# Side work of an attention and FFN kernel placed anew among the main matmuls

## The chip, the cores and the metric

The kernel runs on one core of one Trainium2 chip. The metric is the device time of one execution in microseconds (us), given as the median of several runs. The profile is that of one execution; its times are counted from the start of its span.

## What is computed

Eight batches of an attention over 32 learned slots are followed by a bilinear feed-forward layer. The inputs are q, k, v (8 batches, 8 heads, 576 tokens, 64 wide) and phi (8, 8, 576, 32).

```python
a = np.exp(phi - np.max(phi, axis=2, keepdims=True))
a = a / (np.sum(a, axis=2, keepdims=True) + 1e-09)
k_m = np.einsum('bhsm,bhsd->bhmd', a, k)
v_m = np.einsum('bhsm,bhsd->bhmd', a, v)
scores = (1.0 / np.sqrt(64)) * np.matmul(q, k_m.transpose(0, 1, 3, 2))
attn = softmax(scores)                      # over the 32 slots
x = np.matmul(attn, v_m)                    # to (4608, 512): all heads of a token side by side
out = ((x @ w_a) * (x @ w_b)) @ w_out       # 512 -> 1536 -> 512
```

## The kernel before

The kernel never forms x. It multiplies the 32-slot `v_m` of each head into `w_a` and `w_b` first (the "fold"), so that x @ w_a becomes attn times a folded matrix with 256 rows. For one batch the work on TensorE is this:

- **KV sums** (`kv_sums`, L222): 72 small matmuls in tiles of 64 rows and 32 columns add up `k_m`, `v_m` and the denominators, into two PSUM banks. `take_kv` (L242, units km0 and km1) normalises them on VectorE into `rep` and frees the banks; `rep` is transposed by a DMA on the SP queue (`kv_turn`, unit kvd; batches 4 to 7) or by TensorE (unit kvt; batches 2 and 3).
- **Scores** (`scores`, unit sc, L318): 32 matmuls in tiles of 32*32 into four banks, which ScalarE empties with an exponential (`exp_scores`, units e0 and e1, L331).
- **Normalising** the softmax: for batches up to 3 with TensorE sums, a logarithm and an exponential (units den and nr, L341 to L352); for batches 4 to 7 by turning E with a DMA (unit ed), sums and reciprocals on VectorE (sm0, sm1), products on GpSimd and VectorE (tn0, tn1) and turning it back (ad).
- **Fold** (`fold`, L389): for each third of the 1536 columns (v0, v1, v2) and each of the two weight matrices (a, b), 8 matmuls in 64*32 tiles into two banks. `take_fold` (units x0a to x2b, L402) copies one bank on ScalarE and one on VectorE, or both on ScalarE for the middle third of batches 4 to 7, and frees the two banks. Where one unit folds for both matrices, batches 3 to 7 call `work.settle()` first (L383), which pulls products of the down projection for as long as the flag `brim` says that two of its banks are held at once.
- **Up steps** (`up_half`, L652): twelve steps for each half of a batch's tokens. A step has two matmuls for `pa`, copied on ScalarE to `a_sb` (L663), and two for `pb`, multiplied with it on VectorE into `ht` (L666). These are 128*128 tiles.
- **Down products** (`two_downs`, L518): pairs of 128-token chunks are multiplied with `w_out` in seven products of six matmuls each. Their sums `h_sums` are made ahead by GpSimd (L509), for the last two pairs by VectorE. ScalarE and VectorE put the parts together and SP stores them.

The loop over the batches runs the up steps in order. Behind each half-step `ups` (L677) calls `work.advance()`, which pulls down products at the rate that `work.plan` set for the half, and then the next entry of a list of side units written out by hand: `period[b]`, L755 to L760, with 24 entries for the 24 half-steps of batch b. A unit without a mark belongs to batch b + 1, one with `'` to batch b + 2, one with `_` to batch b. An entry "d5" pulls five more down products, "L6" issues the four input loads of batch 6 (phi, k, v, q; L78, L82, L85, L90) on GpSimd's queue, and "-" does nothing. Units joined by "+" run one after the other within an entry. L753 has such a list for the second half of batch 1.

PSUM banks are dealt out in turn by the class `Banks`: `take` gives the bank that was freed or taken longest ago and isn't held. An entry's place thus sets the order of instructions on every engine, and which bank each later tile gets.

Of the kernel before, what the change touches and what calls it, by code (L numbers as in the profile page):

```python
# [18 lines left out]
def kernel(  # L19
# [72 lines left out]
    def load(b):  # L92
        load_phi(b)
        load_k(b)
        load_v(b)
        load_q(b)
# [571 lines left out]
    def up(b, i, hfs):  # L668
        for hf in hfs:
            up_half(b, i, hf, 0)  # L670
        if len(hfs) > 1:
            yield
        for hf in hfs:
            up_half(b, i, hf, 1)
        yield

    def ups(steps, side=()):  # L677

        side = iter(side)
        for step in steps:  # L680
            for _ in up(*step):
                work.advance()
                next(side, us[step[0]]["-"])()
        for f in side:
            work.advance()
            f()
# [5 lines left out]
    def half_steps(b, hf, lo=0):  # L692

        return [(b, i, (hf,)) for i in range(lo, NFF)]
# [10 lines left out]
    def slots(b, names):  # L705

        def both(fs):
            return lambda: [f() for f in fs]
        def unit(n):
            if n == "fin":  # L710
                return lambda: work.pull(-work.done % NFF)
            if n[0] == "L":
                return lambda: load(int(n[1:]))
            if n[0] == "y":
                return lambda: some(int(n[1:]))
            if n[0] == "d" and n[1:].isdigit():
                return lambda: work.pull(int(n[1:]))
            return us[b + n.endswith("'") - n.endswith("_")][n.rstrip("'_")]

        return [both([unit(n) for n in x.split("+")]) for x in names.split()]  # L720
# [3 lines left out]
    def some(n):  # L724
        for _ in range(n):
            next(early, None)
# [23 lines left out]
    ups(steps(1, 0, 4), slots(1, "d3+y1+hv1a+hx1a hv1b+y3+hx1b - - - y3+v1+x1a+x1b - -"))  # L750
    ups(half_steps(1, 0, 4), slots(1, "- v2+x2a+x2b+qt0' - - qt1'+exp0' exp1'+qt2' - kv'+km'+y9"))
    work.plan(S + HALF, 10)
    ups(half_steps(1, 1, 4), slots(2, "- kvt+qt3 - sc+e0+e1 d1 den0+den1+d1+nr0 - v0a+v0b+nr1+x0a x0b - v1+x1b+x1a -"))  # L753
    period = {}
    period[2] = "v2a_+v2b_+d1+x2a_+L4+x2b_+exp0 - - exp1 kv+km+d1+qt0 - qt1+qt2+d7+kvt - L5+qt3+sc+e0 - d2+v0a+v0b+e1+x0a+x0b - den0+exp0'+d2+d4 v1+nr0+x1a x1b+d10+exp1' - - v2+x2a+x2b+kv' den1+km0' - km1'+kvd'+qt0' - nr1+d4 d5+qt1'+qt2'+qt3' - d6"  # L755
    period[3] = "exp0' sc+exp1'+e0+e1+d3+ed v0b+x0b - v0a+x0a+kv'+km0' km1' d2+sm0+sm1 - kvd' d6+d5+tn1 - tn0+ad v1+x1a+d3 - - x1b L6 qt0' v2+d2+x2a+x2b d1+qt1'+qt2' - - - - qt3'"
    period[4] = "exp0' sc+exp1'+e0+e1+d3+ed - v0a+v0b+x0b+x0a+kv'+km0' km1' - kvd'+d4+d5+sm0+sm1 d2 - d3+tn1 - qt0'+tn0+ad d1+v1+x1a+d3 qt1'+L7 - - - x1b v2a+v2b+x2a+x2b - - d2 - - qt2'+qt3'"
    period[5] = "exp0' sc+exp1'+e0+e1+d3+ed - v0+x0b+x0a+kv'+km0' km1' - d7+sm0+sm1 tn0 d3 d1+kvd'+d5+tn1+d3 - - ad+v1+x1a qt0'+x1b - - - v2+x2b - x2a+qt1' - d2 qt2' qt3' -"
    period[6] = "sc e0+e1+ed - v0+x0b - - sm0 x0a+sm1 d2+v1+d6+x1b+tn1 tn0 ad+d6+x1a - d3 - - - d1 v2+x2a - d3 - x2b+d6 -"
    period[7] = ""  # L760
    for b in range(2, B):
        side = slots(b + 1, period[b])
# [33 lines left out]
```

## Time and profile before

| what | value |
|---|---|
| median of 4 runs | 239.69 us (239.4 to 240.01) |
| the profiled execution | 239.49 us |
| its span | 237.7 us |
| granted TensorE clock, mean | 0.998 |
| up matmuls (L655) | 768, 286 ns each by the trace, next start 122 ns later |
| copies of `pa` (L663, ScalarE) | 192, 409 to 415 ns |
| products into `ht` (L666, VectorE) | 192, 447 to 450 ns |
| fold copies (L402, 512 wide) | ScalarE 52 of 604 ns, VectorE 36 of 685 ns |
| `h_sums` (L509, GpSimd) | 56, 1643 ns |
| out stores (SP) | 68 of 128 KB, 2.7 us to landing |

In lines of the timeline, the first number is the start in us, the second the time from the first start to the last end, then engine, line, operation, what is written from what, tile size, shape and how many. Matmuls are pipelined and overlap, so starts are compared and not durations. In the chain of waits a line has start, duration and what the chain passed through.

### The profile page before, as it was taken

Reading aid. Unit: us, or ns where it says so; the run is one execution under the profiler, and the core shown is the slowest. Engines: PE = TensorE matmul, PEld = TensorE weight load, DVE = VectorE, ACT = ScalarE, POOL = GpSimd, SP = SyncE. Lnnn points to the kernel's source line nnn. Section 1 sums busy time; section 2 is a strip of 40 time slices with the busy share of each in tenths; the row PEclk is TensorE's granted clock in tenths of the full one; section 3 lists DMA queues with packets and bytes.
Section 4 is the critical chain, followed back from the end, with each engine's and each line's share of the span. In section 5 each row is a group of like instructions: output and inputs, shape, how many; then the busy total and the mean of one; then the engine's idle time right before and its main releaser. Section 6 shows DMA issues by size and latency. Waiting matters only on the chain.

```text
span 237.7 us, 7716 instructions
## 1 busy us (share of the span) xinstructions
PE 227.8 (96%) x3064; PEld 167.6 (71%) x3064; DVE 168.5 (71%) x415; ACT 154.2 (65%) x394; POOL 154.7 (65%) x132
## 2 busy tenths in 40 slices
PE   7888998999999999999999999999999999999993
PEld 7645563455756867868777877878687778888882
DVE  3646874368949968979785886779676877756642
ACT  2276761569699489796877458877776777565430
POOL 7954244599979949592889959582929265946001
PEclk9999999999999999999999999999999999999999
DMA  6999999999972999953389959997233260122155
GB/s 233 234 197 206 214 249 207 246 217 276 227 176 64 221 268 237 214 114 74 72 215 208 210 115 201 220 178 100 51 92 70 70 132 8 43 49 68 39 116 134
DMA packets 38437, 37.27 MB, mean 157 GB/s; under 512 B 14689, under 2 KB 32481, under 8 KB 38401
## 3 DMA queue, kind: packets, MB, share of 16 engines
q0 software_dynamic: 19264, 23.14, 52.5%
q1 hardware_dynamic: 18624, 12.85, 24.8%
q10 hardware_dynamic: 512, 0.79, 1.0%
q8 instruction: 24, 0.39, 0.7%
q14 instruction: 13, 0.10, 0.1%
HBM read 42.47 MB, written 9.44 MB: 218 GB/s over the span
## 4 chain that ended last, share of the span: by engine, by line
PE 70%; DMA 16%; POOL 7%; ACT 2%; issue 1%; DVE 1%; DVEq 0%; POOLq 0%
PE py L527 16%; PE pa L655 16%; PE pb L655 15%; PE pv L527 8%; DMA wa_sb<-in_moe_w_a_dram 6%; DMA wo_sb<-in_moe_w_out_dram 6%; PE pva L389 4%; DMA kv_sb<-in_v_dram 4%; PE px L527 4%; PE po L451 3%; PE pkv L222 2%; POOL h_sums L509 2%; POOL wb_sb L100 1%; PE pscore L318 1%; POOL wa_sb L99 1%
## 5 line engine op out<-in xcount | busy, mean ns | idle before, releaser
L666 DVE TENSOR_TENSOR ht<-a_sb,pb 128x288 f16<-128x288 f16 x168 | 72.0, 447 | 34.5 <-ACT a_sb L663 27.7
L655 PEld LDWEIGHTS <-vab 128*128 128x128 f16 x768 | 73.0, 98 | 22.3 <-issue 5.2
L663 ACT CAST a_sb<-pa 128x288 f16<-128x288 f32 x168 | 66.2, 409 | 29.2 <-PE pa L655 25.7
L655 PE MATMUL pa<-A,vab 128*128 128x288 f16 x384 | 75.8, 286 | 0.0
L655 PE MATMUL pb<-A,vab 128*128 128x288 f16 x384 | 75.3, 286 | 0.1
L509 POOL TENSOR_TENSOR h_sums<-ht 128x768 f16<-128x768 f16 x28 | 45.9, 1643 | 28.1 <-DVE ht L666 28.1
L527 PEld LDWEIGHTS <-h_sums 128*128 128x128 f16 x384 | 36.9, 98 | 8.7 <-issue 2.5
L402 ACT CAST vab<-pva 128x512 f16<-128x512 f32 (+1 forms) x60 | 32.0, 574 | 9.5 <-PE pva L389 9.3
L527 PEld LDWEIGHTS <-ht 128*128 128x128 f16 x288 | 27.9, 98 | 6.2 <-issue 1.3
L527 PE MATMUL py<-w_sums,h_sums 128*128 128x256 f16 x192 | 30.0, 273 | 0.0
L402 DVE CAST vab<-pva 128x512 f16<-128x512 f32 (+1 forms) x44 | 27.0, 637 | 4.2 <-PE pva L389 4.0
L509 POOL TENSOR_TENSOR h_sums<-h_sums,ht 128x768 f16<-128x768 f16 x14 | 23.0, 1645 | 1.0
L509 POOL TENSOR_TENSOR h_sums<-ht,h_sums 128x768 f16<-128x768 f16 x14 | 23.0, 1642 | 1.0
L331 ACT ACTIVATE E<-pscore 128x288 f16<-128x288 f32 x32 | 10.8, 418 | 11.1 <-PE pscore L318 10.9
L527 PE MATMUL pv<-w_sums,h_sums 128*128 128x256 f16 x96 | 16.5, 273 | 0.0
L527 PE MATMUL py<-w_sums,ht 128*128 128x256 f16 x96 | 16.2, 273 | 0.1
L534 ACT ACTIVATE u<-py 128x256 f32<-128x256 f32 x32 | 12.5, 391 | 5.8 <-PE py L527 5.3
L527 PE MATMUL py<-wo_sb,ht 128*128 128x256 f16 x96 | 15.9, 273 | 0.0
L527 PE MATMUL pv<-wo_sb,h_sums 128*128 128x256 f16 x96 | 14.9, 272 | 0.0
L527 PE MATMUL px<-wo_sb,ht 128*128 128x256 f16 x96 | 14.9, 273 | 0.0
L205 DVE STREAM_TRANSPOSE qT<-q_sb 128x288 f32<-128x288 f32 x32 | 14.2, 460 | 0.1
L196 ACT ACTIVATE exp_sb<-phi_sb 128x576 f16<-128x576 f32 x16 | 10.9, 696 | 5.2 <-DMA phi_sb<-in_phi_dram 5.2
(71 smaller groups left out, 264.7 us busy)
## 6 DMA issues: line engine op xcount, KB each, us to landing
out_dram<-o_sb SPq DMA_DIRECT2D x68, 128.0 KB, 2.7
phi_sb<-in_phi_dram POOLq DMA_DIRECT2D x8, 576.0 KB, 7.9
kv_sb<-in_v_dram POOLq DMA_DIRECT2D x7, 576.0 KB, 11.7
kv_sb<-in_k_dram POOLq DMA_DIRECT2D x7, 576.0 KB, 11.1
q_sb<-in_q_dram POOLq DMA_DIRECT2D x6, 576.0 KB, 14.3
wo_sb<-in_moe_w_out_dram POOLq DMA_DIRECT2D x6, 256.0 KB, 12.8
q_sb<-in_q_dram POOLq DMA_DIRECT2D x4, 288.0 KB, 11.0
wa_sb<-in_moe_w_a_dram POOLq DMA_DIRECT2D x2, 512.0 KB, 13.9
```

Of the source, the lines that this page charges most:

```text
L196: nc.scalar.activation(out=t["exp"][:, 2 * z:2 * z + 2, :, :], in_=phis[b][:, 2 * z:2 * z + 2, :].rearrange("p c (i m) -> p c i m", m=M), ...
L205: nc.vector.transpose(out=t["qT"][:, hp, :].bitcast(F32), in_=qs[b][:, hp, :].bitcast(F32))
L331: nc.scalar.activation(out=Ev[:, g, :, z, :], in_=pss, func=AF.Exp, scale=1.0 / (8.0 * CS))
L389: nc.tensor.matmul(t["pva", lo, z][g][0][32 * j:32 * j + 32, 0:hi - lo], t["kvT"][64 * r:64 * r + 64, 4 + g, M * j:M * j + M], w_sbs[z][64 ...
L402: engine_copy(out=vabs[b][z][:, g, lo:hi], in_=pva[:, 0:hi - lo])
L451: nc.tensor.matmul(po, ht[:, i, P * c:P * (c + 1)], wo_sb[:, i, :], start=(i == 0), stop=(i == NFF - 1))
L509: engine.tensor_tensor(out=out, in0=in0, in1=in1, op=op)
L527: nc.tensor.matmul(po, lhs[:, i], rhs[:, i], start=first and i == 0, stop=i == KH - 1, skip_group_check=not first)
L534: nc.scalar.mul(out=x, in_=po, mul=scale)
L655: nc.tensor.matmul(ps, vabs[b][x][:, g, P * i:P * (i + 1)], attn[b][:, g, HALF * hf:HALF * (hf + 1)], start=(g == 0), stop=(g == 1))
L663: nc.scalar.copy(out=a_sbs[b, i, hf], in_=ps)
L666: nc.vector.tensor_tensor(out=ht[:, i, t0:t0 + HALF], in0=a_sbs.pop((b, i, hf)), in1=ps, op=ALU.mult)
```

## The change

The entries of `period[2]` to `period[6]` and the list at L753 are placed anew. No unit is added and none is dropped; some pairs of half units are written as one (v0a+v0b as v0, v2a+v2b as v2) or the other way, which decides whether `settle` runs before them, and the numbers of down products pulled at single entries differ. Functions are unchanged.

```diff
-    ups(half_steps(1, 1, 4), slots(2, "- kvt+qt3 - sc+e0+e1 d1 den0+den1+d1+nr0 - v0a+v0b+nr1+x0a x0b - v1+x1b+x1a -"))
+    ups(half_steps(1, 1, 4), slots(2, "- kvt+qt3 - sc+e1+e0 - den0+den1+d1+nr0 - v0+nr1+x0a x0b - v1+x1a+x1b -"))
     period = {}
-    period[2] = "v2a_+v2b_+d1+x2a_+L4+x2b_+exp0 - - exp1 kv+km+d1+qt0 - qt1+qt2+d7+kvt - L5+qt3+sc+e0 - d2+v0a+v0b+e1+x0a+x0b - den0+exp0'+d2+d4 v1+nr0+x1a x1b+d10+exp1' - - v2+x2a+x2b+kv' den1+km0' - km1'+kvd'+qt0' - nr1+d4 d5+qt1'+qt2'+qt3' - d6"
-    period[3] = "exp0' sc+exp1'+e0+e1+d3+ed v0b+x0b - v0a+x0a+kv'+km0' km1' d2+sm0+sm1 - kvd' d6+d5+tn1 - tn0+ad v1+x1a+d3 - - x1b L6 qt0' v2+d2+x2a+x2b d1+qt1'+qt2' - - - - qt3'"
-    period[4] = "exp0' sc+exp1'+e0+e1+d3+ed - v0a+v0b+x0b+x0a+kv'+km0' km1' - kvd'+d4+d5+sm0+sm1 d2 - d3+tn1 - qt0'+tn0+ad d1+v1+x1a+d3 qt1'+L7 - - - x1b v2a+v2b+x2a+x2b - - d2 - - qt2'+qt3'"
-    period[5] = "exp0' sc+exp1'+e0+e1+d3+ed - v0+x0b+x0a+kv'+km0' km1' - d7+sm0+sm1 tn0 d3 d1+kvd'+d5+tn1+d3 - - ad+v1+x1a qt0'+x1b - - - v2+x2b - x2a+qt1' - d2 qt2' qt3' -"
-    period[6] = "sc e0+e1+ed - v0+x0b - - sm0 x0a+sm1 d2+v1+d6+x1b+tn1 tn0 ad+d6+x1a - d3 - - - d1 v2+x2a - d3 - x2b+d6 -"
+    period[2] = "v2_+d1+d1+x2a_+x2b_+L4+exp0 - exp1+qt0 - kv+km+qt1+qt2 d4 d7+kvt - L5+qt3+sc+e1+e0 - d2 exp0' den0+d4+v0b+x0b+d2 d1+v1+nr0+x1a x1b+d10+exp1' - - v2+x2a+kv'+x2b+v0a+x0a - den1+km0' km1'+kvd'+qt0'+qt1' nr1 - d5+qt2'+qt3' - d6+d4"
+    period[3] = "exp0' sc+exp1'+e0+e1+d3+ed - v0a+x0a+kv'+v0b+km0' x0b km1' d5+sm0+kvd'+tn0 - - sm1+d6+d5 tn1+ad - v1+x1a+d3 L6 - x1b - qt0' v2+x2a+d2+x2b - - d4 - qt1'+qt2'+qt3' d1"
+    period[4] = "exp0'+d3 sc+exp1'+e0+e1+ed - v0+x0b+x0a+kv'+d4+km0' km1' - kvd'+d5+sm0+tn0 d2 sm1 - d2+tn1+qt0' qt1'+ad v1+x1a+d3 L7 - - x1b - v2+x2a - - - x2b - qt2'+qt3'"
+    period[5] = "exp0' sc+exp1'+e0+e1+ed+d5 - d3 v0a+v0b+x0b+x0a+kv'+km0' - km1' d8+sm0+tn0 - sm1+d3+d5+kvd' - tn1+v1 x1a+d3 qt0'+x1b - qt1'+d2 ad+d6+d3 - v2+x2a+x2b d4 - - qt2' qt3' -"
+    period[6] = "sc e0+e1+ed - - - - - sm0 - sm1+tn0+d2+v0a+v0b+x0a+x0b+v1+d6+x1b d6 d1+d9 x1a+tn1+ad - - - - - - - - v2+x2a+x2b -"
     period[7] = ""
```

## The prediction, made before the changed kernel ran

> **What bounds the kernel now.** First I read the page's table of busy time, the granted clock and the shares of the chain of waits:
>
> ```profile
> span 237.7 us, 7716 instructions
> PE 227.8 (96%) x3064; PEld 167.6 (71%) x3064; DVE 168.5 (71%) x415; ACT 154.2 (65%) x394; POOL 154.7 (65%) x132
> PEclk9999999999999999999999999999999999999999
> PE 70%; DMA 16%; POOL 7%; ACT 2%; issue 1%; DVE 1%; DVEq 0%; POOLq 0%
> ```
>
> The reader sees TensorE busy in 96% of the span, its clock granted throughout, and no other engine above 71%. From 57 us on the kernel is one stream of matmuls. So a change in the order of work can move the time in two ways only: by what TensorE pays at the seams of its own stream, and by the places where the stream stands still. I read both from TensorE's timeline, first where it changes its tile size (batch 4's two half folds of v0, batch 5's sums):
>
> ```profile
> 103.14 0.41 PE L655 MATMUL pb<-A,vab 128*128 128x288 f16 x2
> 103.48 0.41 PE L389 MATMUL pva<-wb_sb,kvT 64*32 64x512 f16 x8
> 103.82 0.42 PE L655 MATMUL pa<-A,vab 128*128 128x288 f16 x2
> 104.08 0.41 PE L655 MATMUL pb<-A,vab 128*128 128x288 f16 x2
> ...
> 105.23 0.41 PE L389 MATMUL pva<-wa_sb,kvT 64*32 64x512 f16 x8
> 105.46 0.95 PE L222 MATMUL pkv<-kv_sb,exp_sb 64*32 64x192 f16 x72
> 106.34 0.42 PE L655 MATMUL pa<-A,vab 128*128 128x288 f16 x2
> ```
>
> Starts are the thing to read, since durations overlap. A pair of up matmuls with its like behind it takes 0.24 us (103.82 to 104.08 less the 0.02 that follows a switch); the pair at 103.14 takes 0.34 to the fold: 0.10 more. A fold of one weight matrix (8 matmuls) followed by work of the same 64*32 size takes 0.23 (105.23 to 105.46); followed by 128*128 work it takes 0.34: 0.11 more. One visit to the small tile size therefore costs 0.20 us beyond its own work, and work joined to a visit costs nothing extra.
>
> Then the stalls in the region that the change touches:
>
> ```profile
> 85.65 0.41 PE L389 MATMUL pva<-wa_sb,kvT 64*32 64x512 f16 x8
> 85.98 0.41 PE L389 MATMUL pva<-wb_sb,kvT 64*32 64x512 f16 x8
> 86.34 0.41 PE L655 MATMUL pa<-A,vab 128*128 128x288 f16 x2
> ...
> 129.60 0.40 PE L389 MATMUL pva<-wb_sb,kvT 64*32 64x512 f16 x8
> 130.17 0.94 PE L222 MATMUL pkv<-kv_sb,exp_sb 64*32 64x192 f16 x72 [0.17 <-DMA kv_sb<-in_v_dram]
> ```
>
> The folds at 85.65 need 0.33 and 0.36 where 0.23 and 0.34 are enough: 0.12 lost. The fold at 129.60 needs 0.57 for 0.23: 0.34 lost, because the sums of batch 6 wait for v. The chain of waits over that stretch says why v is late:
>
> ```profile
> 115.47 1.65 POOL h_sums L509
> 117.19 1.64 POOL h_sums L509
> 118.82 0.76 POOL phi_sb L78
> 119.58 0.74 POOL kv_sb L82
> 120.31 9.72 DMA kv_sb<-in_v_dram
> ```
>
> GpSimd issues batch 6's loads only after two more h_sums operations. Three further stalls, of about 0.5 (four `pD` matmuls at 67.4), 0.54 (a fold pair that takes 69.88 to 70.97, 1.09 us, against 142.11 to 142.66, 0.55, for one that waits for nothing) and 0.1 us (72.4), lie before the point from which the orders differ in substance.
>
> **The change, part by part.** No instruction is added or dropped: 3064 matmuls stand in both orders, and evictions, loads and stores are only permuted. In the built order of TensorE, tile-size changes number 106 before and 104 after.
>
> *Visits.* Batch 4's two half folds of v0, which the fence shows as two visits, now stand before and behind batch 5's sums: one visit fewer. All other visits are merely moved; the half fold v0a of batch 3 too goes to the far side of a KV visit that exists already. Gain 1 x 0.20 = 0.20 us. This is a plain sum, for nothing hides TensorE's seams.
>
> *Load 6.* In GpSimd's order the four DMA issues of batch 6 (L78, L82, L85, L90) now stand behind the first of the three h_sums operations instead of the third. They go out 2 x 1.72 = 3.4 us earlier (115.47 to 118.82). The transfer of v took 9.72 us, so it lands near 126.6 and not 130.04, with the sums still at 130: the 0.34 us go. The two h_sums operations and the fourth go behind the loads, the former by 4 x 0.75 = 3.0 us. Their users have 4.7 us and more of slack (released 117.11 and 118.82, used 122.39 and 123.53), and the fourth, released at 123.47 and used at 124.68, moves little since loads and sums only swap. Cost 0; if that cover were gone, at most 3.0 - 1.2 = 1.8 us. On SP two or four output stores move ahead of the A transposes of batches 6 and 7; these landed 7.96 and 6.84 us before TensorE took them. Batch 5's E transpose landed at 135.78, 0.03 before VectorE took it, while batch 6's loads ran until 134.71; with these earlier it is not later.
>
> *Batch 3's folds at 85.65.* After the change three more half-steps (some 1.5 us of up and down products) follow the scores before a fold, and all four exponentials run in one piece on ScalarE. Four such took 1.32 us at 102.64, a pitch of 0.30; the products after them hide that. The fold finds its banks empty: gain 0.12. The same swap of e0 and e1 in batch 2 makes the first `pD` wait for the last exponential, and only moves part of a wait that the copy of `a_sb` behind them sets anyway: 0.03 lost.
>
> *New waits.* Three places come out short when evictions are laid end to end. Behind each stands all of TensorE's stream. (a) Batch 3's v2 and its v0a, three half folds, are now evicted in a row; VectorE took 1.28 us for two of 0.68 each at 93.62, a pitch of 0.60. Three take 1.88, and the `ht` next in its queue ends some 0.1 us after TensorE wants its bank. I take 0.12 with the ACT copy in the same place; bounds 0 and one `ht`, 0.45. (b) Batch 4's kvT, already binding by 0.11 at 102.15: its last `rep` now has that extra 0.60 eviction ahead, less the 0.26 in which VectorE was idle before and a 0.36 `ht` that moved behind; nearly even. I take 0.04 lost; bounds -0.11 (wait gone) and 0.3. (c) Batch 4's v0b goes behind batch 5's sums, and the next pairs reuse the banks of `pkv`. These come free 2.06 us after the sums start (105.46 to 107.52, the end of the first two `rep` operations) and are handed over 0.05 later; the `pb` of the second half-step wants one after 0.78 (the sums without their switch) + 0.34 + 0.49 + 0.22 + 0.24 = 2.07. I take 0.05; bounds 0 and 0.45.
>
> *The last batch.* v0 and v1 now stand in one slot, yet not in one run. Before a double fold, `settle` pulls products until PSUM is off its brim, and in the built order 11 products stand between the two runs. There are three visits before and after. Gain 0. The folds come 43 matmuls later for v0 and 34 for v2, and the A transpose 34 later, some 4 us. Its landing had 6.84 us to spare, so about 3 remain: cost 0, and if the cover were gone, no more than the 3 us transfer itself.
>
> Sum: -0.20 - 0.34 - 0.12 + 0.03 + 0.12 + 0.04 + 0.05 = -0.42 us. The profiled execution took 239.49 us (span 237.7 and 1.8 around it), so it would come to 239.07; the median of the four runs is 0.20 above it, and the same sum from 239.69 gives 239.27, rounded 239.3 us.
>
> *The skill against the row.* The row says 0.10 us for each change of tile size. The Trainium skill, "TensorEngine Tiling (Array Packing)", Tiling Modes, says that changing the mode drains the TensorE, and "TensorE: Matmul & The Clock Gate", Single matmul latency, puts a warm matmul's constant part near 166 ns. By that, as an estimate, two changes would bring 0.33 us and the sum would be -0.55. The trace's starts decide. Against the change speaks the first page's section Performance Considerations (PSUM Bottleneck): tiling speeds TensorE up but not the emptying of PSUM. Longer runs in small tiles are what it warns of; by it the three new waits would lie at their upper bounds.
>
> **Rivals.** *All stalls go, none comes.* Without the four new losses (0.24) and with the kvT wait of 0.11 gone: -0.20 - 0.34 - 0.12 - 0.11 = -0.77, 238.9 us. For it: the three new waits are each around 0.1, less than a transfer or a queue may shift. Against: VectorE is without idle time around 94 to 98 us.
>
> *The runs wait for PSUM (slower).* A longer run takes up to six banks of eight while two ACT and two DVE copies per pair empty them. Its price is the row at 69.88: 0.54 us a run. Four runs are longer or lie closer (batch 3's v2 with v0a, batch 4's v0 with the sums, batch 7's v0 and v1). Against the 0.66 of gains it decides from the second wait on; with three, 3 x 0.54 - 0.66 = +0.96, 240.65 us. Against it: runs of 16 at 142, 147 and 171 us pass without a wait.
>
> *It does not do what it says.* Only one visit is saved, as counted. If besides v lands no earlier, because the transfer, not the issue, is limited, what is left is -0.42 + 0.34 = -0.08: 239.6 us. For it: the v of batch 5 took 14.7 us from issue to landing, which from 116.9 would be too late. Against it: that one ran behind batch 4's loads; the v of batch 4 took 10.7, and even 12 would be in time.
>
> **How the numbers follow.** About 0.2%, 0.48 us, is what a measurement of this kernel can tell from no change. My forecast, -0.42, has 0.52 and lies just inside that; its own range is 238.9 to 239.6, and a quarter of it (0.13) is beyond -0.48. The first rival has 0.26, the second 0.10, the third 0.12. Faster: 0.13 + 0.26 = 0.39; same: 0.39 + 0.12 = 0.51; slower: 0.10. The range runs from the first rival less the spread of the runs (0.3) to the new waits near their upper bounds (0.45 + 0.3 + 0.45 in place of 0.21 gives +0.57): 238.6 to 240.2.
>
> **What would show it.** The sums of batch 6 0.23 us behind the fold before them, with no wait on in_v; batch 3's folds at 0.23 and 0.34; batch 4's half folds around batch 5's sums with no switch between. A new wait shows as an up pair longer than 0.25 just behind the sums of batches 4 and 5. Wrong I would be if a fold takes 0.5 again past 75 us, if TensorE waits for h_sums near 122, or if batch 7's first up waits for A.

## The result, and the profile after

| kernel | median | runs | lowest to highest |
|---|---|---|---|
| before | 239.73 us | 53 | 239.12 to 240.92 |
| after | 239.11 us | 32 | 238.76 to 240.53 |

The ratio of after to before is 0.9978, with a 95% interval of 0.997 to 0.9986: 0.53 us less, between 0.34 and 0.72. The same kernel run a second time, on another occasion, gave 238.97 us and a ratio of 0.9972 (0.996 to 0.9983). The profiled execution of after took 239.16 us with a span of 237.5; that of before had 239.49 and 237.7. So the two profiles differ by 0.33 where the medians differ by 0.62, and to find out why is the main part of what follows.

The head of the page of after, with the shares of the chain of waits:

```profile
span 237.5 us, 7718 instructions
PE 227.3 (96%) x3064; PEld 167.7 (71%) x3064; DVE 169.5 (71%) x415; ACT 153.5 (65%) x394; POOL 155.6 (66%) x132
PEclk9999999999999999999999999999999999999999
PE 76%; DMA 14%; POOL 5%; ACT 2%; issue 1%; DVE 1%; DVEq 0%; POOLq 0%
```

The same matmuls, the same clock, and busy shares within one point. GpSimd (POOL) has gone from 7% to 5% of the chain, since its loads of batch 6 no longer stand there. The rest is read from TensorE's timeline, first around batch 4's scores and batch 5's sums:

```profile
101.91 0.27 PE L527 MATMUL py<-w_sums,ht 128*128 128x256 f16 x1
102.58 0.48 PE L318 MATMUL pscore<-qT,kvT 32*32 32x288 f16 x32 [0.40 <-DMA kvT<-rep]
...
104.62 0.41 PE L389 MATMUL pva<-wa_sb,kvT 64*32 64x512 f16 x8
104.85 0.97 PE L222 MATMUL pkv<-kv_sb,exp_sb 64*32 64x192 f16 x72
105.59 0.44 PE L389 MATMUL pva<-wb_sb,kvT 64*32 64x512 f16 x8
105.96 0.42 PE L655 MATMUL pa<-A,vab 128*128 128x288 f16 x2
...
106.68 0.41 PE L655 MATMUL pa<-A,vab 128*128 128x288 f16 x2
107.04 0.42 PE L655 MATMUL pb<-A,vab 128*128 128x288 f16 x2
```

Fold, sums and fold are one visit now: 104.62 to 105.96, 1.34 us. Before, the same work took 0.10 (switch) + 0.34 + 0.23 + 0.88 = 1.55 in two visits. That is 0.21 less, as foreseen (0.20). The pair at 106.68 needs 0.36 to its partner where 0.24 is enough: the bank wait (c), 0.11. TensorE's weight loads (PEld) at that place name what ended it, one of VectorE's `rep` operations:

```profile
107.04 0.11 PEld L655 LDWEIGHTS <-vab 128*128 128x128 f16 x2 [0.26 <-DVE rep L254]
```

The wait (a) stands behind batch 3's `pD` matmuls:

```profile
95.36 0.41 PE L341 MATMUL pD<-E,ones 128*128 128x288 f16 x2
95.69 0.41 PE L655 MATMUL pa<-A,vab 128*128 128x288 f16 x2
```

The 0.33 between them is 0.09 more than the 0.24 that is enough; the `ht` operation behind VectorE's three fold copies ended at 95.64, just before. And the scores of batch 4 start 0.67 after the product before them, where a product and a change of size take 0.20: they wait 0.47 for kvT, where before they waited 0.11.

Batch 3's first fold, and the sums of batch 6, in the same view:

```profile
87.52 0.41 PE L389 MATMUL pva<-wb_sb,kvT 64*32 64x512 f16 x8
87.87 0.39 PE L527 MATMUL px<-wo_sb,ht 128*128 128x256 f16 x2
...
129.84 0.40 PE L389 MATMUL pva<-wb_sb,kvT 64*32 64x512 f16 x8
130.05 0.95 PE L222 MATMUL pkv<-kv_sb,exp_sb 64*32 64x192 f16 x72
```

Both stalls are gone: 0.35 to the next work of another size, and 0.21 from fold to sums. For the sums, GpSimd's timeline shows why:

```profile
114.24 1.64 POOL L509 TENSOR_TENSOR h_sums<-ht 128x768 f16<-128x768 f16 x1 [2.28 <-DVE ht L666]
115.82 0.81 POOL L78 DMA_DIRECT2D phi_sb<-in_phi_dram  x1
116.62 0.75 POOL L82 DMA_DIRECT2D kv_sb<-in_k_dram  x1
117.36 0.75 POOL L85 DMA_DIRECT2D kv_sb<-in_v_dram  x1
```

v is issued at 117.36 instead of 120.31. Its transfer took 11.09 us instead of 9.72 and landed at 128.44, 1.61 us before the sums began.

### The profile page after: what moved, and what is told of

Read it like the earlier page. It is cut to its first block, busy times and chain, and to the rows that moved or that the text cites. A ratio compares the mean times of both kernels' runs of the same rounds, so it can differ in the third digit from the quotient of the medians.

```text
span 237.5 us, 7718 instructions
## 1 busy us (share of the span) xinstructions
PE 227.3 (96%) x3064; PEld 167.7 (71%) x3064; DVE 169.5 (71%) x415; ACT 153.5 (65%) x394; POOL 155.6 (66%) x132
## 4 chain that ended last, share of the span: by engine, by line
PE 76%; DMA 14%; POOL 5%; ACT 2%; issue 1%; DVE 1%; DVEq 0%; POOLq 0%
PE py L527 17%; PE pa L655 17%; PE pb L655 17%; PE pv L527 8%; DMA wa_sb<-in_moe_w_a_dram 6%; DMA wo_sb<-in_moe_w_out_dram 6%; PE pva L389 5%; PE px L527 4%; PE po L451 3%; PE pkv L222 2%; DMA kvT<-rep 2%; PE pscore L318 1%; POOL wb_sb L100 1%; POOL wa_sb L99 1%; POOL kv_sb L168 1%
## 5 line engine op out<-in xcount | busy, mean ns | idle before, releaser
L509 POOL TENSOR_TENSOR h_sums<-ht 128x768 f16<-128x768 f16 x28 | 46.7, 1669 | 23.4 <-DVE ht L666 23.4
L527 PE MATMUL px<-wo_sb,ht 128*128 128x256 f16 x96 | 15.9, 273 | 0.0
L527 PE MATMUL py<-w_sums,ht 128*128 128x256 f16 x96 | 15.2, 272 | 0.1
L527 PE MATMUL pv<-wo_sb,h_sums 128*128 128x256 f16 x96 | 14.4, 272 | 0.0
L196 ACT ACTIVATE exp_sb<-phi_sb 128x576 f16<-128x576 f32 x16 | 10.9, 700 | 5.2 <-DMA phi_sb<-in_phi_dram 5.2
```

What stands on the lines that cost most here:

```text
L196: nc.scalar.activation(out=t["exp"][:, 2 * z:2 * z + 2, :, :], in_=phis[b][:, 2 * z:2 * z + 2, :].rearrange("p c (i m) -> p c i m", m=M), ...
L509: engine.tensor_tensor(out=out, in0=in0, in1=in1, op=op)
L527: nc.tensor.matmul(po, lhs[:, i], rhs[:, i], start=first and i == 0, stop=i == KH - 1, skip_group_check=not first)
```

## The experiments

Each row gives the ratio to the kernel before with its 95% interval, from 11 or 12 runs of the kernel. Runs e0, e1, e2 and e4 were measured together on one chip, e3, e5, e6 and e7 on a second, e8 to e10 on a third, e11 on a fourth, each time beside the kernel before; so medians are compared within these groups, and ratios across them.

| run | what | median | ratio |
|---|---|---|---|
| e0_after_again | after, once more | 238.97 | 0.9972 (0.996 to 0.9983) |
| e1_load6_late | after, loads of batch 6 late | 239.71 | 1.0006 (0.9995 to 1.0016) |
| e2_load6_early | before, loads of batch 6 early | 239.22 | 0.9986 (0.9976 to 0.9997) |
| e3_one_visit | before, one visit fewer | 239.77 | 1.0016 (1.0002 to 1.0031) |
| e4_km_early | after, batch 4's rep early | 239.56 | 1.0006 (0.999 to 1.0022) |
| e5_visit_load6 | before, both of e2 and e3 | 239.34 | 0.9993 (0.9984 to 1.0001) |
| e6_last_run | after, last folds really in one run | 240.12 | 1.0024 (1.0015 to 1.0033) |
| e7_scores_later | after, batch 4's scores later | 239.65 | 1.0005 (0.9991 to 1.0019) |
| e8_visit_undone | after, the saved visit undone | 239.23 | 0.9978 (0.996 to 0.9995) |
| e9_q5_late | after, q of batch 5 loaded late | 238.95 | 0.9961 (0.9941 to 0.9981) |
| e10_q_late | as e9, q of batches 6 and 7 too | 239.68 | 0.9995 (0.997 to 1.0021) |
| e11_q5_fill | as e9, products behind the sums | 239.23 | 0.9985 (0.9971 to 0.9998) |

The lists hold 23 to 26 entries; what stands beyond the 24th runs behind the last half-step. To compare profiles, each is cut into stretches by TensorE's starts: from the pair at 58.9 us (up to there all orders are alike) to where batch 4's scores could start; the wait for kvT; from the scores to the fold before batch 6's sums; the wait for v; and the rest to the last matmul. A wait is the distance of two starts less what it is without a wait (0.20 from a product to scores, 0.22 to 0.23 from fold to sums, so the columns are good to 0.02). The sum without the waits is what the order itself costs. The stretch up to the pair at 58.9, which is left out, ended between 58.74 and 59.04 in these profiles, whatever the order.

| profile (us) | to scores | kvT wait | to batch 6's fold | v wait | rest | sum without waits |
|---|---|---|---|---|---|---|
| before | 43.11 | 0.11 | 27.47 | 0.34 | 103.55 | 174.13 |
| e2 | 43.11 | 0.33 | 27.48 | 0 | 103.54 | 174.12 |
| e3 | 43.11 | 0.23 | 27.58 | 0.21 | 103.58 | 174.27 |
| e5 | 43.30 | 0.69 | 27.55 | 0 | 103.55 | 174.40 |
| after | 43.19 | 0.47 | 27.28 | 0 | 103.48 | 173.95 |
| e0 | 43.19 | 0.22 | 27.28 | 0 | 103.49 + 0.18 | 173.96 |
| e1 | 43.19 | 0.23 | 27.28 | 0.58 | 103.49 | 173.96 |
| e8 | 43.20 | 0.60 | 27.36 | 0 | 103.55 | 174.11 |
| e9 | 43.19 | 0 | 27.46 | 0 | 103.55 | 174.20 |

Two things belong to the reading of this table. The changed order has one matmul of the down products (0.11) more ahead of the scores and one fewer between them and batch 6's fold, so its 0.08 more and 0.19 less in these stretches are 0.03 less and 0.08 less for the same work. And e5 has TensorE's order of e3, yet took 0.19 more up to the scores: in its scores at 83.83 TensorE pauses for 0.2 and waits for nothing that the profile shows. So the sum without waits is not free of scatter.

**The changed kernel once more (e0).**

> The changed kernel once more, as the measure for the three kernels that run beside it. The profile of it that I have is 239.16 us; its TensorE starts differ from the profile of before by -0.20 (visit), -0.34 (sums of batch 6), -0.12 (batch 3's folds), +0.36 (scores of batch 4 wait for kvT), +0.09 and +0.11 (two bank waits), +0.03: about -0.07, while the medians differ by about 0.6. Theory A: the waits for transfers (v of batch 6 before, kvT of batch 4 after) differ from execution to execution, and the profiles showed a mild v wait and a long kvT wait; then this profile's kvT wait is well under 0.47, and the ratio to before is again near 0.9978. Theory B: the waits are fixed by the order and the 0.6 comes from somewhere else; then the kvT wait is 0.45 to 0.5 again with the same ratio.

Theory A. The order's own cost is the same to 0.01 us in three profiles of after's TensorE order (after, e0 and e1: 173.95, 173.96, 173.96), while the kvT wait was 0.47, 0.22 and 0.23. The 0.18 is a wait that the first profile didn't have: v of batch 7 took 13.4 us and landed at 157.80, with the sums at 157.93.

**Load 6 alone, undone and done (e1, e2).**

```diff
 period[3], after -> e1
-v1+x1a+d3 L6 - x1b - qt0' v2+x2a
+v1+x1a+d3 - - x1b L6 qt0' v2+x2a
 period[3], before -> e2
-v1+x1a+d3 - - x1b L6 qt0' v2+d2
+v1+x1a+d3 L6 - x1b - qt0' v2+d2
```

> The changed kernel with the four loads of batch 6 issued behind the third h_sums again, as before; nothing else differs. Theory (the earlier issue is what took the wait of batch 6's sums away, worth 0.34): the sums wait for v again by 0.3 to 0.4, time +0.3 us against the changed kernel, ratio to before near 0.999. Rival 1 (the wait varies widely and costs more on average than the profile of before showed): +0.4 to +0.6. Rival 2 (the transfer, not the issue, sets when v lands, or the gain is given back in the tail): within 0.1 of the changed kernel.

> The kernel before with only the loads of batch 6 moved up, to where the change has them. Theory: the fold before batch 6's sums is followed by them after 0.23 and not 0.57, time -0.34 us against before (ratio 0.9986). Rival 1 (the wait costs more on average): -0.5 to -0.6, which would be nearly all of what the change brought. Rival 2 (the issue does not matter): 0.

The issue decides, not the transfer: rival 2 falls in both. The chain of waits of e1 (start, duration, what it passed through) has the loads in it again:

```profile
113.92 1.65 POOL h_sums L509
115.64 1.66 POOL h_sums L509
117.36 1.65 POOL h_sums L509
119.01 0.75 POOL phi_sb L78
119.75 0.74 POOL kv_sb L82
120.49 9.65 DMA kv_sb<-in_v_dram
130.28 0.94 PE pkv L222 x72
```

The timeline of e1, and below it that of e2:

```profile
129.47 0.40 PE L389 MATMUL pva<-wb_sb,kvT 64*32 64x512 f16 x8
130.28 0.52 PE L222 MATMUL pkv<-kv_sb,exp_sb 64*32 64x192 f16 x32 [0.41 <-DMA kv_sb<-in_v_dram]
```

```profile
129.85 0.40 PE L389 MATMUL pva<-wb_sb,kvT 64*32 64x512 f16 x8
130.07 0.95 PE L222 MATMUL pkv<-kv_sb,exp_sb 64*32 64x192 f16 x72
```

0.81 from fold to sums in e1, 0.22 in e2. In e2 the loads alone brought 0.14%, 0.34 us (0.07 to 0.57), the forecast's very number. In e1 they cost more than that, 239.71 - 238.97 = 0.74, and its profile shows a wait of 0.58 instead of 0.34. v was issued there, counted from the pair at 58.9, 0.3 later than before. e1 lies nearer to rival 1, and beyond it. Its ratio, 1.0006, does not mean that the other moves bring nothing, since its v wait is 0.24 longer than before's. What the median of e1 has beyond its profiled execution (239.71 against 239.44) no profile shows.

**The visit, on the kernel before (e3, e5).**

```diff
 period[3], before -> e3 (e5: L6 as in e2, too)
-v0b+x0b - v0a+x0a+kv'+km0' km1' d2
+- - v0a+x0a+kv'+v0b+km0' x0b+km1' d2
```

> The kernel before with v0b of batch 3 moved behind batch 5's sums, as the change has it: one visit to the small tile size fewer, loads of batch 6 left late. Theory 1 (places add): -0.20 for the visit, +0.05 to +0.11 for the bank wait behind the sums, so -0.10 to -0.15 against before (0.9995). Theory 2 (v of batch 6 lands at a time that TensorE's pace does not move, as the runs before suggest: the changed kernel with the late loads took as long as before): TensorE comes to batch 6's sums 0.1 to 0.2 earlier, the wait for v grows by as much (0.34 to about 0.5), and the time is that of before within 0.1.

> Both parts on the kernel before: the one visit fewer and the loads of batch 6 earlier. Theory 1 (places add): -0.40 (as measured for the loads alone) -0.10 to -0.15, about -0.5. Theory 2 (the late v swallows what is gained before it, the early one lets it through): the same -0.5 to -0.6, but here the visit is worth more than it is alone: the difference from the loads alone is 0.1 to 0.2, where with the late loads it is 0 to 0.1. Rival (the rest of what the change brought comes from other moves): the same as with the loads alone, -0.4.

(The v0b that the first of these texts, and that of e8 below, count to batch 3 stands in `period[3]` and folds for batch 4.) Nothing here tells the two theories apart: both had e3 at the time of before or below, and its ratio says 0.38 us more (0.05 to 0.74), of which the profile shows 0.14 in the order. The edit puts x0b and km1' into one entry, which the change does not, and the timeline of e3 shows what that costs:

```profile
108.53 0.41 PE L655 MATMUL pa<-A,vab 128*128 128x288 f16 x2
109.02 0.41 PE L655 MATMUL pb<-A,vab 128*128 128x288 f16 x2
```

0.49 where 0.24 is enough: 0.25 lost to a bank that VectorE empties late (a `rep` operation ends at 108.97, just before), more than the visit's 0.20. The stretch from the scores to batch 6's fold is 0.1 longer than before, not shorter. TensorE did not come to the sums early, so whether a late v swallows earlier gains was not tested. With the early loads, in e5, the visit in this form brings nothing over e2 either (0.9993 against 0.9986, the intervals overlap).

**The visit undone (e8).**

```diff
 period[3], after -> e8
-sc+exp1'+e0+e1+d3+ed - v0a+x0a+kv'+v0b+km0' x0b km1'
+sc+exp1'+e0+e1+d3+ed v0b+x0b v0a+x0a+kv'+km0' - km1'
```

> The changed kernel with its one saved visit undone: v0b of batch 3 stands in a visit of its own again, ahead of v0a and batch 5's sums. 106 changes of tile size in place of 104; everything else, the early loads too, as in the changed kernel. Theory (a visit costs 0.20 and the bank wait behind the sums, 0.06 to 0.11 in three profiles of the changed kernel's order, goes with it): +0.1 to +0.15 against the changed kernel, ratio to before about 0.998; the half folds each take 0.34 to the 128*128 work behind them. Rival 1 (the visit is worth more, since it brings evictions and banks apart): +0.3 or more. Rival 2 (the visit is worth nothing once its bank wait is paid): 0 or below.

Without its waits, e8 takes 0.15 us more than after's order (174.11 against 173.96), 0.08 of it in the stretch with the visit and 0.07 in the rest behind it, where the order is the same and profiles scatter by as much. The stall at 106.8 is gone. So this visit costs 0.20 by the fences, the one bank wait that saving it brings takes back up to half, and about 0.1 remains (0.08 in this pair of profiles). The ratio, 0.9978, can't tell that from nothing; its profile had the longest kvT wait of this order, 0.60.

**The last batch in one run (e6).**

```diff
 period[6], after -> e6
-v0a+v0b+x0a+x0b+v1+d6+x1b
+v0a+v0b+x0a+x0b+v1a+v1b+d6+x1b
```

> The changed kernel with the last batch's v1 written as v1a+v1b, so that no down products are pulled between v0 and v1 and both really stand in one run: 102 changes of tile size in place of 104. Theory (a visit costs 0.20 and nothing else stops): -0.20. Rival 1 (four half folds take eight banks, and the run waits for its evictions): one or two fold pairs there take 0.5 to 1.1 where 0.23 is enough, time +0.3 to +0.9. Rival 2 (half of each): within 0.1 of the changed kernel.

Rival 1. The timeline of e6:

```profile
186.22 0.41 PE L389 MATMUL pva<-wa_sb,kvT 64*32 64x512 f16 x8
186.44 0.40 PE L389 MATMUL pva<-wb_sb,kvT 64*32 64x512 f16 x8
186.66 0.40 PE L389 MATMUL pva<-wa_sb,kvT 64*32 64x512 f16 x8
187.33 0.37 PE L389 MATMUL pva<-wb_sb,kvT 64*32 64x512 f16 x1 [0.27 <-ACT vab L402]
187.90 0.41 PE L389 MATMUL pva<-wb_sb,kvT 64*32 64x512 f16 x7 [0.20 <-DVE vab L402]
```

The third half fold takes 0.67 to the fourth where 0.23 is enough, and the fourth, broken after its first matmul, 0.91 to the products at 188.24 where 0.34 is: 0.44 + 0.57 lost, waiting for the copies on ScalarE and VectorE, and 0.10 more in an up pair at 190.2. Less the 0.20 of the visit that is 0.91 (the rest behind the v wait is 0.90 longer than after's, 104.38 against 103.48); by the ratios e6 is 1.1 to 1.25 us slower than after and e0, so 0.2 to 0.3 of it is not in this profile. So "two folds of the last batch in one run" would have been a loss; the change is spared it because `settle`, which v1 as one unit calls, pulls 11 products in between.

**Attempts on the kvT wait (e4, e7).**

```diff
 period[2], after -> e4
-- den1+km0' km1'+kvd'+qt0'+qt1' nr1
+km0' den1+km1'+kvd' qt0'+qt1' nr1
 period[3] and period[4], after -> e7
-exp0' sc+exp1'+e0+e1+d3+ed -
+exp0' - sc+exp1'+e0+e1+d3+ed -
...
-d5+sm0+kvd'+tn0 - - sm1+d6+d5
+d5+sm0+kvd'+tn0 - sm1+d6+d5
...
-qt1'+ad v1+x1a+d3 L7 - - x1b
+qt1'+ad+L7 v1+x1a+d3 - - - x1b
```

> The changed kernel with batch 4's km0, km1 and kvd one half-step earlier, so that its kvT is issued 0.5 to 0.9 us sooner; TensorE's order is the same. Theory (the scores of batch 4 wait 0.47 for kvT in every execution, because TensorE now arrives earlier): the wait goes to under 0.1, time -0.3 to -0.45 us against the changed kernel, about 238.75. Rival 1 (the long wait was that of one profiled execution): -0.1 or less. Rival 2 (the rep operations ahead of the ht products on VectorE take the place of the wait): two up pairs near 97 us lose 0.3 or more and the time is the same or longer.

> The changed kernel with the scores of batch 4, and what follows them up to the normalising, one half-step later (one empty entry less behind them), and the loads of batch 7 one half-step earlier. TensorE has then some 0.6 us of up products to do while kvT of batch 4 is on its way, and v of batch 7 lands before 157. Theory (the wait for kvT of 0.2 to 0.5 is in every execution, that for v of batch 7 of up to 0.2 in some): -0.2 to -0.4 against the changed kernel, about 238.7. Rival 1 (the exponentials and the folds behind them then wait for banks): the same or longer by up to 0.3. Rival 2 (the wait moves on to a later transfer, the turned E or the v of batch 6): stalls of the same size at 123 or 130, no gain.

Both took the wait away and both lost by it, 0.6 us (e4, by the medians) and 0.8 (e7, by the ratios) against e0. In e4 the wait came back as one for banks. Its timeline around 96 us, VectorE's lines among TensorE's:

```profile
95.77 0.41 PE L655 MATMUL pa<-A,vab 128*128 128x288 f16 x2
95.83 0.74 DVE L254 TENSOR_SCALAR rep<-pkv,rphi 128x256 f16<-128x256 f32 x2
96.49 0.45 DVE L666 TENSOR_TENSOR ht<-a_sb,pb 128x288 f16<-128x288 f16 x1
96.63 0.41 PE L655 MATMUL pb<-A,vab 128*128 128x288 f16 x2 [0.45 <-DVE rep L254]
```

The bank that TensorE wants next is now one that the two rep operations empty. They end at 96.57, TensorE goes on at 96.63, and 0.61 is lost; the pair behind batch 5's sums, at 107.4, loses 0.28 in the same way. That is rival 2, with one long and one short wait in place of two near 97. kvT was issued only 0.4 earlier (97.86 against 98.25; 0.5 counted from the pair at 58.9). In e7 the up pair behind the sums waits 0.28 for `rep`, a fold pair at 113.5 0.11 and the up pair at 114.8 0.29 for `ht`: rival 1.

**What holds kvT up (e9, e10, e11).**

```diff
 e9: load(5) without its load_q; a new unit Q5 = load_q(5) in period[3]
-x0b km1' d5+sm0+kvd'+tn0
+x0b km1'+Q5 d5+sm0+kvd'+tn0
 e10: Q6 and Q7 too, in the first entries of period[4] and period[5]
 e11: e9, and in period[3]
-v0a+x0a+kv'+v0b+km0' x0b km1'+Q5 d5+sm0
+v0a+x0a+kv'+v0b+km0'+d3 x0b km1'+Q5 d2+sm0
```

> The changed kernel with the fourth load of batch 5 (q) issued some 21 us later, at 105; it was issued at 84.3 and landed at 101.4, 16.9 us before its first use, while kvT of batch 4 was on its way (98.1 to 102.2). Order on TensorE unchanged. Theory (kvT takes 4.0 to 4.6 us because loads are in flight; kvT of batch 5 took 2.74 with none): kvT of batch 4 lands 0.8 us or more sooner, its wait of 0.2 to 0.7 goes, time -0.2 to -0.45 against the changed kernel, ratio about 0.996. Rival 1 (the latency of a turn near 100 us has another cause, the out stores): kvT 4 us as before, no gain. Rival 2 (TensorE comes earlier and then waits for banks behind the exponentials or the sums): kvT lands sooner, no gain.

> As the run before, with the q loads of batches 6 and 7 late as well (issued near 125 and 152 in place of 118 and 145; first used at 139.7 and 168.6). Theory: v of batches 6 and 7 lands 1 to 2 us sooner after its issue (10.9 to 13.4 us so far), so that the occasional wait of batch 7's sums (0.18 in one profile) goes too; another -0.05 to -0.15. Rival (the late q loads collide with the turned E of batches 5 and 6 and TensorE waits for scores or A): a stall near 140 or 170, +0.3.

> As the run with the q load of batch 5 late, and three of the five down products of a later entry pulled right behind the sums and the half fold, so that TensorE has 0.33 us of work that needs no new bank while the banks of pkv and pva are emptied. Theory (the 0.28 that the up pair at 106.4 waited there is all that swallowed the gain of the early kvT): no stall over 0.1 near 102 and 106.5, time -0.2 to -0.3 against that run, 238.7, ratio to before about 0.995. Rival (emptying the banks is what limits the stretch, so the stall only moves to the next half-steps): a stall of 0.2 to 0.3 at 107 to 109, time as in that run.

The answer of the tile view on kvT around 100 us, for e0 and below it for e9 (whose lines are numbered one higher; the 0.4 is the idle time of the weight load ahead of the scores, 0.22 of which delayed them):

```profile
L268 SPq DMA_TRANSPOSE kvT<-rep x1: 1317/1317/1317, 98.1 to 98.1; - x1
...
  DMA kvT<-rep: 0.4, 1
...
DMA to landing us min/median/max: 4.0/4.0/4.0
```

```profile
L269 SPq DMA_TRANSPOSE kvT<-rep x1: 1312/1312/1312, 98.3 to 98.3; - x1
...
DMA to landing us min/median/max: 2.9/2.9/2.9
```

This is shown: with q of batch 5 out of the way kvT takes 2.9 us (e9, e10 and e11) instead of 4.0 to 4.6 (eleven profiles), and the scores wait for no DMA. The out stores are not the cause: none is issued between 92.5 and 103 us in e0 or in e9. The late q load then meets the next transfer of this kind: it is in flight from 106.75 to 112.99, and batch 5's kvT, issued at 108.96, takes 4.8 us (e9 and e10) where it took 2.7 in the eleven profiles without such a load. Nobody waits for that one. But for batch 4 TensorE comes to the up pair behind the sums that much earlier, and in e9's timeline:

```profile
106.29 0.41 PE L656 MATMUL pa<-A,vab 128*128 128x288 f16 x2
...
106.81 0.11 PEld L656 LDWEIGHTS <-vab 128*128 128x128 f16 x2 [0.42 <-DVE rep L255]
106.81 0.42 PE L656 MATMUL pb<-A,vab 128*128 128x288 f16 x2
```

0.52 where 0.24 is enough. Theory and rival 2 were both right: the wait for kvT is replaced by a wait for the bank that VectorE's rep operations free, 0.28 instead of 0.05 to 0.11. Counted from the pair at 58.9, the second of them ends at 47.78 in e9 and at 47.81 in e0, so VectorE has no use for TensorE's coming 0.22 earlier. By this pair the first 0.2 of a kvT wait costs nothing in this order. e11 fills that place with products, and the stall only splits, 0.16 at 106.5 and 0.16 at 108.8, much as its rival had it: emptying the banks limits this stretch. By the ratios e9 is the fastest of all, but its interval overlaps after's, so nothing here is shown to beat the changed kernel. e10 has a profile like e9's, but its twelve runs fall into two groups, six from 238.75 to 239.27 and six from 240.10 to 240.72; the profile is of the first, and what the second is stays open.

## Why the prediction was right

The time, 239.11, lies 0.2 below the forecast of 239.3 and within the range. The range, 238.6 to 240.2, also held the time of before, so it is the steps that test the forecast:

| term | predicted | measured |
|---|---|---|
| one visit fewer | -0.20 | -0.21 by the fences (0.33, the other price that was named, is too high) |
| loads of batch 6 | -0.34 | -0.34 in the profiles; -0.34 (0.07 to 0.57) in e2; 0.74 between e0 and e1 |
| batch 3's folds | -0.12 | -0.12 |
| swap of e0 and e1 in batch 2 | +0.03 | +0.03 in the first pair |
| (a) three half folds evicted in a row | +0.12 | +0.09 |
| (b) kvT of batch 4 | +0.04 | +0.06 by issue and arrival; +0.36 in the first pair of profiles; see below |
| (c) v0b behind batch 5's sums | +0.05 | +0.05 to +0.11 (after, e0, e1, e6); 0.28 where kvT is not waited for (e4, e7, e9, e10) |

The visit, the loads and kvT have runs of their own; the folds, the swap and (a) were not tried alone, and their numbers are read from the profiles.

**The first reading of (b) was wrong.** With 0.36 the terms come to -0.05, and the medians say -0.5 to -0.6. But most of that wait is not the order's: kvT's latency varied from 4.0 to 4.6 us whatever the order. What the order itself moves can be read without it: counted from the pair at 58.9, kvT is issued at 39.2 in the old order (before, e2, e3) and 0.14 later in the new, and TensorE could start the scores 0.08 later. That leaves +0.06 for the term, which was +0.04. Four profiles of the old order up to there (before, e2, e3, e5) waited 0.11, 0.33, 0.23 and 0.69, mean 0.34; five of the new (after, e0, e1, e6, e8) 0.47, 0.22, 0.23, 0.34 and 0.60, mean 0.37. By these means the term is +0.03, with 0.2 of scatter in one execution and so some 0.15 in the difference. The two profiles compared first happened to have the shortest wait of the one and a long one of the other.

**The sum then closes, with what scatters left out.** The order itself became 174.13 - 173.96 = 0.17 shorter (the visit, the folds, the swap, (a) and (c) were forecast at -0.20 - 0.12 + 0.03 + 0.12 + 0.05 = -0.12). Of this 0.11 lies before batch 6's sums, where these terms are, and 0.06 in the rest, where none was foreseen and where e8 and e9, with after's order, took as long as before. The v wait, 0.34, 0.58 and 0.21 in three profiles with late loads, mean 0.37, is 0 in all with early ones. With +0.03 for kvT that is -0.17 - 0.37 + 0.03 = -0.51, or -0.45 without the rest; measured -0.53 (0.34 to 0.72) and -0.67 (0.41 to 0.96). Both intervals hold the forecast's -0.42 as well. What the median has beyond it is too small to be given to single terms, and whether the second median's -0.67 holds anything more is open.

**The forecast's weak step was its base**, not its mechanism: it took the stalls of one execution (a kvT wait of 0.11, the least of four) as those of every execution. It also had no term for v of batch 7, which is waited for at times (0.18 in e0); its issue moved from 144.21 to 144.77 in the profiles (0.57 later counted from the pair at 58.9, 0.33 later in e0).

**The rivals.** *All stalls go, none comes* fell: two new bank waits did come, (a) and (c), and the kvT wait stayed. *The runs wait for PSUM* fell for the change as it is, but e6 shows that its price of 0.54 a run was no exaggeration for a run that is long enough: 0.44 + 0.57 in a single run of 32 fold matmuls. The Trainium skill, "TensorEngine Tiling (Array Packing)", Performance Considerations (PSUM Bottleneck), warns that tiling speeds TensorE up but not the emptying of PSUM, without a length of run at which this begins; e6 agrees, where TensorE waits for copies on both engines, and so do e4, e7, e9 and e11, where each gain came back as a wait for VectorE. *It does not do what it says* was half right on the last batch, as foreseen (no run, no gain), and wrong on load 6: its transfer took 10.9 to 12.3 us instead of 9.5 to 9.7 when issued earlier, yet landed in time, twice only 0.2 us before the sums began (e6, e7), where 0.13 is the least that was seen (before, e1, e3, which waited).

Of the signs of being wrong none showed: past 75 us no fold took 0.5 and TensorE did not wait for h_sums near 122. The A transpose of batch 7 landed at 197.44, 3.4 us before the first matmul that reads it, where about 3 were foreseen.

## What to carry to other kernels

A wait for a transfer is a draw, not a constant: before a difference between two profiles is put down to a change, take the waits out of both, compare what is left (here it repeated to 0.01 us in three profiles and was off by 0.1 to 0.2 in others), and then compare the waits over several executions. A load that lands at the last moment in one profile is worth issuing earlier: here that was the largest single gain, and the wait was gone in all eleven profiles with the early issue. A load that nobody waits for yet can slow a transfer that somebody does wait for; moving it pays only if nothing else is the next limit, and here VectorE was. Joining small tiles into longer visits pays 0.1 us a change here, but only while the engines that empty the banks are not already the next limit: look for who frees the bank behind the visit before counting the gain.

## What the hardware showed that was not expected

The turn of kvT, the same instruction on the same queue, took 2.7 us to landing with no loads in flight (batch 5's, at 109 us), 2.9 where the load of v ended at 98.9 and q's came later (e9), and 4.0 to 4.6 with q's load in flight until 101.3 to 102.1, though that is on another queue. It goes the other way round too: batch 5's own kvT took 4.8 when q's load was moved onto it (e9, e10). And batch 6's, near 134 us, took 4.4 to 4.8 in the three profiles where q of batch 6 was in flight for another 0.6 us or more (before, e1, e3), and 2.7 to 3.1 in the seven where q had landed 2 us or more ahead (e0, e2, e4, e5, e8, e9, e11); three where q landed within 0.5 us of the issue took 3.4 to 3.9 (e6, e7, e10). The Trainium skill, "DMA: Bandwidth & Descriptors", Queues, rings and completion order, says that each of the DMA engines takes turns between the queues that have work for it, packet by packet; the runs agree as far as they go, since taking away a load on GpSimd's queue made a transfer on SP's faster by 1.1 us. The same v load took 9.5 to 9.7 us issued at 120.5 and 10.9 to 12.3 issued at 117.4; why the earlier one is slower was not tried.
